# Second block's softmax on VectorE, low parts later, a fifth buffer for gated tiles: a fused attention and gating kernel

## The chip, the cores and the metric

The kernel runs on one core of a Trainium2 chip. Measured is the device time of one execution, in microseconds (us). A run gives one time; several runs of the same kernel are compared by their median. One further execution was profiled, and all rows below come from it.

## The reference

Attention inside chunks of 64 tokens, then two dense layers with a gate, then two more with a squared clip:

```python
scores = scale * np.matmul(q_c, k_c.transpose(0, 1, 2, 4, 3))   # chunks of 64, D = 64, 8 heads
scores = scores - np.max(scores, axis=-1, keepdims=True)
attn = np.exp(scores)
attn = attn / (np.sum(attn, axis=-1, keepdims=True) + 1e-09)
out = np.matmul(attn, v_c)
# x: 4608 tokens x 512 (heads side by side)
gate = 1.0 / (1.0 + np.exp(-(x @ w_gate)))                       # 512 -> 1536
val = x @ w_val
y = gate * val @ w_out                                           # 1536 -> 512
h = y @ w_in                                                     # 512 -> 2048
g = np.where(h >= 1, h, np.where(h <= -1, 0.0, (h + 1) ** 2 / 4))
return g @ w_out2                                                # 2048 -> 512
```

Inputs and output are float32.

## The kernel before

**Numbers.** Matrix products run on float32 operands that are split into a high and a low part. `three` issues three matmuls for one product (high by high, high by low, low by high; the lines L501, L502 and L503). `x` is the high part, a copy on ScalarE (L419), and `l` the low part, a subtraction on VectorE (L423).

**Blocks.** The 4608 tokens are nine blocks of 512. For every block the first stage computes the attention of its four pairs of heads, and then 12 pairs of products of 512 columns: gate, sigmoid on ScalarE (L905), value, and the product of both on VectorE (L908) into the tile `sg`, which SyncE (SP) stores to DRAM (`gT`, L791). One gate or value product is 12 matmuls of 128x512. Later stages read `gT` and compute the other three layers; they are not touched by the change and begin at about 745 us.

**Slots.** The first stage is written as a program by slots. A block has NS = 24 slots; each is one gate or value product on TensorE, gate in the even and value in the odd slots. `at(slot, prio, fn)` books a step, and `emit(slot)` writes all booked steps of that slot ahead of its product, by fraction of the slot, then by `prio`. What each engine runs, and in which order, follows from that alone: an engine takes its instructions in the written order, and waits for semaphores at each. All DMAs are issued by SP in the written order too.

**Attention beside the products.** `first_block` computes block 0's attention alone (0 to 36 us). For the others, `later_block(b, starts, when)` books the steps of pair p at slot `starts[p]` plus an offset for each of `tsmenwpcoxl`: transposes of q and k on VectorE (t, L306), scores on TensorE (s, L323), maximum (m), exponential on ScalarE (e), sums and reciprocal on VectorE (n), scaling of the weights on GpSimd (w, L383), transposes on TensorE (p, L389), their copy on ScalarE (c, L392), product with v on TensorE (o, L403), high parts (x), low parts (l). Loads of q and k are booked with `starts[p - 1]` (L281, 16 DMAs for a pair in blocks 1 to 7), those of v with `starts[p]` (L296). Block 1, the second, is computed beside block 0's products, in which VectorE, ScalarE and GpSimd also convert the weights (L111, L117, L124, L128, L137, L138).

**Softmax of block 1 before.** Only this block has a form of its own. `m_scaled` takes the maxima on VectorE (L347) and multiplies them by -scale (L348). `e_sums` runs eight exponentials of 128x64 on ScalarE straight from the scores, each with its maximum as the bias and each summing its row (L359). All other blocks subtract the maxima on VectorE (L339, four instructions), take one exponential of 128x512 (L367) and sum on VectorE (L375).

**Buffers.** The tile `sg` has four buffers, so the sigmoid of product pair f writes the buffer of pair f-4 and waits until that store has landed. The store of pair f, whose gate is in slot 2f, is booked in slot 2f + 4.

**Weights of later stages.** From slot 26 on, weights of the later layers are loaded (L102, L106), converted and written back to DRAM (L182), also by SP, beside the attention.

Of the kernel before, what the change touches and what calls it, by code (L numbers as in the profile page):

```python
# [8 lines left out]
F32 = mybir.dt.float32  # L9
F32R = mybir.dt.float32r  # L10
# [3 lines left out]
AF = mybir.ActivationFunctionType  # L14
ALU = mybir.AluOpType
AX = mybir.AxisListType
# [12 lines left out]
def kernel(  # L29
# [207 lines left out]
    class Whole:  # L237
# [88 lines left out]
            self.B["s", p] = banks  # L326

        def m(self, p):
            if self.b == 1:
                return self.m_scaled(p)  # L330
            s = self.SP[p][:, 0].rearrange("p (g h k) -> p g h k", h=2, k=CH)
            m = cp.tile([P, 2, NC], F32, tag="m0", name="m", bufs=2)
            banks = self.B.pop(("s", p))
            for h, b in enumerate(banks):
                nc.vector.tensor_reduce(out=m[:, h], in_=b, axis=AX.X, op=ALU.max)
            for h, b in enumerate(banks):
                for swap in range(2):
                    gs = slice(swap * NC // 2, (swap + 1) * NC // 2)
                    nc.vector.tensor_tensor(  # L339
                        out=s[:, gs, h ^ swap], in0=b[:, gs],  # L340
                        in1=m[:, h, gs].unsqueeze(2).to_broadcast([P, NC // 2, CH]), op=ALU.subtract,
                    )

        def m_scaled(self, p):
            m = cp.tile([P, 2, NC], F32, tag="m1", name="m", bufs=2)
            for h, b in enumerate(self.B["s", p]):
                nc.vector.tensor_reduce(out=m[:, h], in_=b, axis=AX.X, op=ALU.max)  # L347
            nc.vector.tensor_scalar_mul(m, m, -scale)  # L348
            self.B["m", p] = m

        def e_sums(self, p):

            s = self.SP[p][:, 0].rearrange("p (g h k) -> p g h k", h=2, k=CH)
            self.B["l", p] = l = cp.tile([P, NC, 2], F32, tag="l1", name="l", bufs=2)
            m = self.B.pop(("m", p))
            for h, b in enumerate(self.B.pop(("s", p))):
                for g in range(NC):
                    r = h ^ (g >= NC // 2)
                    nc.scalar.activation(  # L359
                        s[:, g, r], b[:, g], AF.Exp, bias=m[:, h, g:g + 1], scale=scale,  # L360
                        accum_out=l[:, g, r:r + 1],
                    )

        def e(self, p):
            if self.b == 1:
                return self.e_sums(p)
            nc.scalar.activation(self.SP[p][:, 0], self.SP[p][:, 0], AF.Exp, scale=scale)  # L367

        def n(self, p):
            if self.b == 1:  # L370
                l = self.B.pop(("l", p)).rearrange("p g h -> p (g h)")
            else:
                s = self.SP[p][:, 0].rearrange("p (g k) -> p g k", k=CH)
                l = cp.tile([P, 2 * NC], F32, tag="l0", name="l", bufs=2)
                nc.vector.tensor_reduce(out=l, in_=s, axis=AX.X, op=ALU.add)  # L375
            nc.vector.tensor_scalar_add(l, l, 1e-9)
            self.B["r", p] = r = cp.tile([P, 2 * NC], F32, tag="r0", name="r", bufs=2)
            nc.vector.reciprocal(out=r, in_=l)
# [46 lines left out]
    def first_block():  # L425
# [24 lines left out]
                    wl(1)  # L450
                n -= fn not in (w_low, w_bits)

        z = pool["sg"].tile([P, BS], F32R, tag="sg", name="z", bufs=4)
        nc.vector.memset(f32(z), 0.0)
        kv_["ident"] = cp.tile([P, P], F32, name="ident")
        make_identity(nc, kv_["ident"])
# [25 lines left out]
    def later_block(b, starts, when):  # L482

        bufs = {"qk": 2, "qkT": 1, "sp": 2, "vd": 2}

        def alloc(nm):
            cols = BS // 2 if nm == "vd" else BS
            return pool["u"].tile([P, 2, cols], F32, tag=nm, name=nm, bufs=bufs[nm])

        a = Whole(b, [None, "b4", "b5", "b6", "b6", "b7"], alloc, "V" * KT)  # L490
        for p, s0 in enumerate(starts):
            at(starts[p - 1] + 0.5 if p else s0 - 6, 5, a.load, p)
            at(s0 + 0.5, 5, a.v_load, p)
            for fn, dt in zip("tsmenwpcoxl", when):
                at(s0 + dt, {"s": 0, "p": 0, "o": 0, "m": 1, "e": 1, "c": 1, "x": 1}.get(fn, 3), getattr(a, fn), p)
# [294 lines left out]
    def g_store(b, f, sg):  # L790
        nc.sync.dma_start(out=gT[b][f * P:(f + 1) * P, :], in_=sg)  # L791

    later_block(1, [5 * p for p in range(KT)], (0, 1, 1.5, 2, 3, 3, 5, 5.5, 7, 7.5, 8))
    for b in range(2, NB):
        later_block(
            b, [NS * (b - 1) + 6 * p - 6 for p in range(KT)], (0, 2, 3, 3.5, 4, 4.5, 6, 7, 8, 9, 10)
# [83 lines left out]
    with tc.manual_schedule():  # L880
# [18 lines left out]
        for b in range(NB):  # L899
            for f in range(F1):  # L900
                slot = NS * b + 2 * f
                emit(slot)
                go = proj(("g", f), b, f"b{f % 2}")
                sg = pool["sg"].tile([P, BS], F32, tag="sg", name="sg", bufs=4)
                nc.scalar.activation(sg, go, AF.Sigmoid)  # L905
                emit(slot + 1)
                vo = proj(("v", f), b, f"b{2 + f % 2}")
                nc.vector.tensor_tensor(out=sg, in0=vo, in1=sg, op=ALU.mult)  # L908
                at(slot + 4, 7, g_store, b, f, sg)
        for t in range(3):  # L910
            emit(NS * NB + t)
        close_pool("sg")
        assert not ev, ev
# [38 lines left out]
```

## Time and profile before

| | us |
|---|---|
| median of 3 runs | 1727.68 |
| lowest, highest | 1726.67, 1732.06 |
| the profiled execution | 1730.08 |
| its span, from first to last instruction | 1728.3 |
| TensorE busy | 1658.0 |
| VectorE, ScalarE, GpSimd busy | 1188.6, 876.9, 834.6 |
| mean granted clock of TensorE | 0.988 |

Matmuls overlap in TensorE, so its busy time says when it is not idle, not that it runs at its peak. In the rows, PE is TensorE, PEld its weight loads, DVE VectorE, ACT ScalarE, POOL GpSimd and SPq the queue of SyncE. `L423` is line 423 of the kernel. "A <- B" in a wait is: A stood idle until B had ended.

### The profile page before, as it was taken

Reading aid. Unit: us, or ns where it says so; the run is one execution under the profiler, and the core shown is the slowest. Engines: PE = TensorE matmul, PEld = TensorE weight load, DVE = VectorE, ACT = ScalarE, POOL = GpSimd, SP = SyncE. Lnnn points to the kernel's source line nnn. Section 1 sums busy time; section 2 is a strip of 40 time slices with the busy share of each in tenths; the row PEclk is TensorE's granted clock in tenths of the full one; section 3 lists DMA queues with packets and bytes.
Section 4 is the critical chain, followed back from the end, with each engine's and each line's share of the span. In section 5 each row is a group of like instructions: output and inputs, shape, how many; then the busy total and the mean of one; then the engine's idle time right before and its main releaser. Section 6 shows DMA issues by size and latency. Waiting matters only on the chain.

```text
span 1728.3 us, 30194 instructions
## 1 busy us (share of the span) xinstructions
PE 1658.0 (96%) x10695; PEld 1525.4 (88%) x10695; DVE 1188.6 (69%) x1856; ACT 876.9 (51%) x1694; POOL 834.6 (48%) x755
## 2 busy tenths in 40 slices
PE   5889999998999899999999999999999999999998
PEld 4668887776877788899999999999999999999998
DVE  5875556555555562178777767888787879788876
ACT  5664455444454453145555555555554455545453
POOL 1431433433333241057777753533450476777675
PEclk8899999999999999999999999999999999999999
DMA  7655767777776875834654654333427954463452
GB/s 209 189 128 135 214 176 215 214 210 205 197 204 186 241 225 172 320 105 152 218 158 145 240 216 153 122 134 138 156 102 278 345 194 115 114 183 109 120 138 37
DMA packets 385991, 307.16 MB, mean 178 GB/s; under 512 B 267696, under 2 KB 298928, under 8 KB 385840
## 3 DMA queue, kind: packets, MB, share of 16 engines
q1 hardware_dynamic: 385840, 305.23, 57.6%
q8 instruction: 84, 1.38, 0.3%
q14 instruction: 67, 0.55, 0.1%
HBM read 179.83 MB, written 125.30 MB: 177 GB/s over the span
## 4 chain that ended last, share of the span: by engine, by line
PE 77%; DMA 8%; SPq 7%; DVE 4%; ACT 2%; issue 2%; POOL 1%; DVEq 0%; ACTq 0%; POOLq 0%
PE P L502 18%; PE P L503 18%; PE P L501 18%; PE pr L501 7%; PE pr L502 7%; PE pr L503 7%; SPq L281 4%; DMA gT<-sg 2%; SPq L296 2%; DMA raw<-in_moe_w_gate_dram 1%; PE O L403 1%; DMA raw<-in_moe_w_in_dram 1%; DMA vd<-in_v_dram 1%; DVE z L534 1%; PE S L323 1%
## 5 line engine op out<-in xcount | busy, mean ns | idle before, releaser
L545 POOL TENSOR_TENSOR z<-z 128x384 fp32r<-128x384 f32 x305 | 355.9, 1189 | 313.7 <-ACT z L538 306.6
L502 PE MATMUL P<-z,w 128*128 128x384 f32 x1344 | 454.6, 338 | 4.1 <-POOL z L545 2.2
L501 PE MATMUL P<-z,w 128*128 128x384 f32 x1344 | 453.7, 338 | 0.0
L503 PE MATMUL P<-z,w 128*128 128x384 f32 x1344 | 453.4, 337 | 0.0
L501 PE MATMUL pr<-x,w 128*128 128x512 f32 x864 | 347.9, 403 | 0.0
L502 PE MATMUL pr<-x,w 128*128 128x512 f32 x864 | 340.5, 394 | 0.9 <-DVE x L423 0.9
L503 PE MATMUL pr<-x,w 128*128 128x512 f32 x864 | 339.9, 393 | 0.0
L538 ACT ACTIVATE z<-z 128x384 fp32r<-128x384 f32 x420 | 206.0, 521 | 178.9 <-DVE z L534 108.6
L545 POOL TENSOR_TENSOR op<-in,op 128x384 fp32r<-128x384 f32 x168 | 191.0, 1155 | 147.6 <-ACT op L538 146.9
L502 PEld LDWEIGHTS P<-z,w 128*128 128x128 f32 x1344 | 252.5, 188 | 7.2 <-POOL z L545 5.0
L501 PEld LDWEIGHTS P<-z,w 128*128 128x128 f32 x1344 | 252.4, 188 | 0.6 <-ACT z L538 0.2
L503 PEld LDWEIGHTS P<-z,w 128*128 128x128 f32 x1344 | 252.4, 188 | 0.0
L908 DVE TENSOR_TENSOR sg<-pr,sg 128x512 f32<-128x512 f32 x108 | 74.5, 690 | 257.4 <-PE pr L503 108.6
L905 ACT ACTIVATE sg<-pr 128x512 f32<-128x512 f32 x108 | 64.6, 598 | 300.3 <-PE pr L503 215.9
L501 PEld LDWEIGHTS pr<-x,w 128*128 128x128 f32 x864 | 164.7, 191 | 35.3
L503 PEld LDWEIGHTS pr<-x,w 128*128 128x128 f32 x864 | 164.3, 190 | 35.4
L502 PEld LDWEIGHTS pr<-x,w 128*128 128x128 f32 x864 | 164.7, 191 | 33.6 <-DVE x L423 1.4
L538 ACT ACTIVATE op<-in 128x384 fp32r<-128x384 f32 x252 | 128.5, 523 | 112.3 <-PE P L503 57.7
L534 DVE TENSOR_TENSOR z<-z 128x384 f32<-128x384 f32 x200 | 168.5, 892 | 1.0 <-POOL z L545 0.9
L502 PE MATMUL P<-op,w 128*128 128x384 f32 x504 | 168.5, 334 | 0.1
L501 PE MATMUL P<-op,w 128*128 128x384 f32 x504 | 168.5, 334 | 0.0
L503 PE MATMUL P<-op,w 128*128 128x384 f32 x504 | 168.4, 334 | 0.0
(68 smaller groups left out, 2257.4 us busy)
## 6 DMA issues: line engine op xcount, KB each, us to landing
uT<-ua SPq DMA_DIRECT2D x96, 384.0 KB, 2.3
z<-uT SPq DMA_DIRECT2D x96, 384.0 KB, 4.3
gT<-sg SPq DMA_DIRECT2D x108, 256.0 KB, 5.1
in<-gT SPq DMA_DIRECT2D x72, 256.0 KB, 3.9
raw<-in_moe_w_out_dram SPq DMA_DIRECT2D x28, 512.0 KB, 6.4
w<-swi SPq DMA_DIRECT2D x28, 512.0 KB, 5.7
w<-swp SPq DMA_DIRECT2D x28, 512.0 KB, 6.9
swi<-st SPq DMA_DIRECT2D x24, 512.0 KB, 4.1
```

Of the source, the lines that this page charges most:

```text
L281: nc.sync.dma_start(out=t[32 * g:32 * g + 32, i, off // 32:(off + m) // 32], in_=rows[h, :, 32 * j:32 * j + 32].rearrange("(t i) r -> i t ...
L296: nc.sync.dma_start(out=t[heads[h ^ swap], lo // CH:hi // CH], in_=v[bb, 2 * p + h, s0 + lo - off:s0 + hi - off].rearrange("(c k) d -> k c ...
L323: nc.tensor.matmul(banks[h][heads[c % 2], c // 2], lhsT=t[hs, 0, ts], rhs=t[hs, 1, ts], start=True, stop=True)
L403: nc.tensor.matmul(banks[r][heads[r ^ swap], g_, i], lhsT=self.V[p][rows, c], rhs=self.SP[p][rows, 1, chunks[c]], start=True, stop=True,)
L501: nc.tensor.matmul(o, lhsT=ah, rhs=bh, start=first, stop=False, skip_group_check=open_)
L502: nc.tensor.matmul(o, lhsT=ah, rhs=bl, start=False, stop=False, skip_group_check=open_)
L503: nc.tensor.matmul(o, lhsT=al, rhs=bh, start=False, stop=last, skip_group_check=open_)
L534: (eng or nc.vector).tensor_tensor(out=op_src(p, key), in0=x, in1=y, op=ALU.subtract)
L538: nc.scalar.activation(o[:, 0], op_src(p, key), AF.Copy)
L545: eng.tensor_tensor(out=o[:, 1], in0=op_src(p, key), in1=f32(o[:, 0]), op=ALU.subtract)
L905: nc.scalar.activation(sg, go, AF.Sigmoid)
L908: nc.vector.tensor_tensor(out=sg, in0=vo, in1=sg, op=ALU.mult)
```

## The change

Three things. Block 1's softmax takes the form of the other blocks: `m_scaled` and `e_sums` go. The tile `sg` (and `z`, which shares its buffers) has five buffers instead of four, and its store is booked in slot 2f + 3 instead of 2f + 4. In block 1 the last pair starts at slot 14 instead of 15, and the low parts of each pair come at offset 9 instead of 8.

```diff
         def m(self, p):
-            if self.b == 1:
-                return self.m_scaled(p)
...
-        def m_scaled(self, p):
-            m = cp.tile([P, 2, NC], F32, tag="m1", name="m", bufs=2)
-            for h, b in enumerate(self.B["s", p]):
-                nc.vector.tensor_reduce(out=m[:, h], in_=b, axis=AX.X, op=ALU.max)
-            nc.vector.tensor_scalar_mul(m, m, -scale)
-            self.B["m", p] = m
-
-        def e_sums(self, p):
...
-                    nc.scalar.activation(
-                        s[:, g, r], b[:, g], AF.Exp, bias=m[:, h, g:g + 1], scale=scale,
-                        accum_out=l[:, g, r:r + 1],
-                    )
...
-        z = pool["sg"].tile([P, BS], F32R, tag="sg", name="z", bufs=4)
+        z = pool["sg"].tile([P, BS], F32R, tag="sg", name="z", bufs=5)
...
-    later_block(1, [5 * p for p in range(KT)], (0, 1, 1.5, 2, 3, 3, 5, 5.5, 7, 7.5, 8))
+    later_block(1, [0, 5, 10, 14], (0, 1, 1.5, 2, 3, 3, 5, 5.5, 7, 7.5, 9))
...
-                sg = pool["sg"].tile([P, BS], F32, tag="sg", name="sg", bufs=4)
+                sg = pool["sg"].tile([P, BS], F32, tag="sg", name="sg", bufs=5)
...
-                at(slot + 4, 7, g_store, b, f, sg)
-        for t in range(3):
+                at(slot + 3, 7, g_store, b, f, sg)
+        for t in range(2):
```

VectorE, block 0, the second pair of block 1 and the low parts of the first, before:

```order
L347 TENSOR_REDUCE m<-S 128x4 x2
L348 TENSOR_SCALAR m<-m 128x8
L128 SCALAR_TENSOR_TENSOR raw<-raw 128x512
L111 TENSOR_SCALAR raw<-raw 128x512
L117 SCALAR_TENSOR_TENSOR raw<-raw 128x512
L908 TENSOR_TENSOR sg<-pr,sg 128x512
L423 TENSOR_TENSOR x<-O,x 64x256 x4
L376 TENSOR_SCALAR l<-l 128x8
L378 RECIPROCAL r<-l 128x8
L128 SCALAR_TENSOR_TENSOR raw<-raw 128x512
```

and after, where the lines are numbered lower (L333 and L337 are the maxima and the subtraction, L348 to L351 sum and reciprocal, L396 the low parts, L881 the gated product):

```order
L333 TENSOR_REDUCE m<-S 128x4 x2
L337 TENSOR_TENSOR sp<-S,m 128x2x64 x4
L128 SCALAR_TENSOR_TENSOR raw<-raw 128x512
L111 TENSOR_SCALAR raw<-raw 128x512
L117 SCALAR_TENSOR_TENSOR raw<-raw 128x512
L881 TENSOR_TENSOR sg<-pr,sg 128x512
L348 TENSOR_REDUCE l<-sp 128x8
L349 TENSOR_SCALAR l<-l 128x8
L351 RECIPROCAL r<-l 128x8
L128 SCALAR_TENSOR_TENSOR raw<-raw 128x512
L111 TENSOR_SCALAR raw<-raw 128x512
L117 SCALAR_TENSOR_TENSOR raw<-raw 128x512
```

The low parts have moved behind the sum, the reciprocal and one more weight (the next row after these is L396).

SP's queue, block 0, around the loads for the second and third pair of block 1 (gT_66 is block 0's), before:

```order
L102 DMA raw<-in_moe_w_val_dram 128x4x128
L791 DMA gT_66<-sg 128x512
L102 DMA raw<-in_moe_w_gate_dram 128x4x128
L296 DMA vd<-in_v_dram 64x64 x2
L296 DMA vd<-in_v_dram 64x3x64 x2
L296 DMA vd<-in_v_dram 64x4x64 x2
L281 DMA qk<-in_q_dram 32x2x32 x4
```

and after:

```order
L764 DMA gT_66<-sg 128x512
L102 DMA raw<-in_moe_w_val_dram 128x4x128
L102 DMA raw<-in_moe_w_gate_dram 128x4x128
L764 DMA gT_66<-sg 128x512
L296 DMA vd<-in_v_dram 64x64 x2
L296 DMA vd<-in_v_dram 64x3x64 x2
L296 DMA vd<-in_v_dram 64x4x64 x2
L281 DMA qk<-in_q_dram 32x2x32 x4
```

The store of product pair 1, which stood behind six loads of v, 16 of q and k and a weight, now stands ahead of them.

## Rows read from the trace of the kernel before

**Rows 1.** Busy time by engine, behind the first stretches: stretch, length, engine busy.

```profile
582.00:750.00 168.00, 168.00 (x1019) 139.02 (x1019) 61.56 (x124) 59.20 (x104) 39.83 (x40) 1.00 0.70 230
```

**Rows 2.** Waits of TensorE, 36 to 130 us: total, times, longest.

```profile
PE S L323 <- DVE qkT L306: 9.9, 4, 5.0
PE PT L389 <- POOL sp L383: 7.4, 3, 2.6
```

**Rows 3.** VectorE's waits, 36 to 130 us; timeline rows of one period: start, duration.

```profile
DVE x L423 <- ACT x L419: 13.2, 4, 3.9
...
71.37 0.51 DVE L348 TENSOR_SCALAR m<-m 128x8 f32<-128x8 f32 x1
...
77.95 1.53 DVE L423 TENSOR_TENSOR x<-O,x 64x256 fp32r<-64x256 f32 x4 [3.56 <-ACT x L419]
...
80.05 1.38 POOL L383 TENSOR_TENSOR sp<-sp,r 128x512 f32<-128x512 f32 x1 [2.47 <-DVE r L378]
```

**Rows 4.** Waits of TensorE and of ScalarE, 250 to 582 us.

```profile
PE O L403 <- ACT sp L392: 23.4, 10, 4.8
...
ACT sg L905 <- DMA gT<-sg: 84.0, 14, 10.4
```

**Rows 5.** Waits of SP, 36 to 152 us; the last row 152 to 600 us.

```profile
SPq L791 <- DVE sg L908: 5.3, 2, 3.4
...
SPq L791 <- DVE m L335: 2.8, 1, 2.8
...
SPq L296 <- PE O L403: 1.0, 1, 1.0
...
SPq L791 <- DVE sg L908: 1.5, 3, 0.7
```

**Rows 6.** Timeline of SP, block 6: start, duration, issues.

```profile
552.49 5.65 SPq L296 DMA_DIRECT2D vd<-in_v_dram  x6
558.18 4.08 SPq L281 DMA_DIRECT2D qk<-in_q_dram  x8
...
567.74 1.20 SPq L791 DMA_DIRECT2D gT<-sg  x2
```

**Rows 7.** Groups by line (busy us, mean ns): ScalarE and VectorE, 36 to 582 us.

```profile
L359 ACT ACTIVATE sp<-S,m 128x64 f32<-128x64 f32 x32 | 9.6, 324 | 0.0
...
L367 ACT ACTIVATE sp<-sp 128x512 f32<-128x512 f32 x23 | 14.6, 633 | 0.3
...
L339 DVE TENSOR_TENSOR sp<-S,m 128x128 f32<-128x128 f32 x96 | 20.9, 278 | 0.0
...
L375 DVE TENSOR_REDUCE l<-sp 128x8 f32<-128x512 f32 x23 | 15.8, 686 | 2.7 <-ACT sp L367 1.8
```

**Rows 8.** Busy time in two stretches; third last number: TensorE's granted clock.

```profile
103.20:106.60 3.40, 3.28 (x10) 2.80 (x11) 3.24 (x4) 0.70 (x1) 1.50 (x2) 0.50 0.81 183
574.30:581.10 6.80, 6.29 (x74) 5.27 (x75) 3.53 (x9) 1.59 (x3) 1.95 (x3) 0.50 0.91 257
```

**Rows 9.** Timeline of SP, six v pieces at two places; the product of pair 1.

```profile
55.56 6.76 SPq L296 DMA_DIRECT2D vd<-in_v_dram  x6
...
62.45 0.68 DVE L908 TENSOR_TENSOR sg<-pr,sg 128x512 f32<-128x512 f32 x1
...
132.28 3.88 SPq L296 DMA_DIRECT2D vd<-in_v_dram  x6
```

**Rows 10.** Timeline of VectorE, TensorE and ScalarE around the last long wait.

```profile
549.21 0.71 DVE L306 STREAM_TRANSPOSE qkT<-qk 128x512 f32<-128x512 f32 x1 [2.35 <-DMA qk<-in_k_dram]
...
552.05 0.65 PE L323 MATMUL S<-qkT 64*64 64x64 f32 x32
...
573.67 0.60 ACT L905 ACTIVATE sg<-pr 128x512 f32<-128x512 f32 x1 [10.36 <-DMA gT<-sg]
...
574.81 1.14 PE L403 MATMUL O<-sp,vd 64*64 64x64 f32 x32 [4.54 <-ACT sp L392]
...
581.80 0.60 ACT L905 ACTIVATE sg<-pr 128x512 f32<-128x512 f32 x1 [5.91 <-PE pr L503]
```

More of the change, by code (lines that the diff above doesn't have):

```diff
@@ L342, in m @@
                     )
-        def m_scaled(self, p):
-            m = cp.tile([P, 2, NC], F32, tag="m1", name="m", bufs=2)
-            for h, b in enumerate(self.B["s", p]):
-                nc.vector.tensor_reduce(out=m[:, h], in_=b, axis=AX.X, op=ALU.max)
-            nc.vector.tensor_scalar_mul(m, m, -scale)
-            self.B["m", p] = m
-        def e_sums(self, p):
[L353 to L358, printed above, removed]
-                    nc.scalar.activation(
-                        s[:, g, r], b[:, g], AF.Exp, bias=m[:, h, g:g + 1], scale=scale,
-                        accum_out=l[:, g, r:r + 1],
-                    )
         def e(self, p):
-            if self.b == 1:
-                return self.e_sums(p)
             nc.scalar.activation(self.SP[p][:, 0], self.SP[p][:, 0], AF.Exp, scale=scale)
         def n(self, p):
[L370 to L375, printed above, removed]
+            s = self.SP[p][:, 0].rearrange("p (g k) -> p g k", k=CH)
+            l = cp.tile([P, 2 * NC], F32, tag="l0", name="l", bufs=2)
+            nc.vector.tensor_reduce(out=l, in_=s, axis=AX.X, op=ALU.add)
             nc.vector.tensor_scalar_add(l, l, 1e-9)
```

## The prediction

> **What bounds the kernel now.** I read the waits of TensorE by stretch first, then asked for each waiting engine what it waits for, and ended at the queue of SP, which issues every DMA. TensorE stands idle in two stretches of the attention-and-gating stage only; behind 582 us it is busy in all of 168 us [rows 1], so work before that point shifts the end one for one if it shifts TensorE at all.
>
> First stretch, 36 to 130 us (block 0, with the attention of the second block beside it): TensorE waits 9.9 us for the transposed q and k and 7.4 us for the weights that GpSimd has scaled [rows 2]. What ends these waits is VectorE's order. In one period it stands 3.56 us before the low parts (L423), because the copies of the high parts (L419) stand behind the exponentials on ScalarE; four such waits make 13.2 us; only then come the sums' small operations and the scaling on GpSimd at 80.05 [rows 3], on which TensorE waits three times, 7.4 / 3 = 2.5 us each [rows 2].
>
> Second stretch, 250 to 582 us: TensorE waits 23.4 us for the copy L392, ten times, and that copy stands behind sigmoids that wait 84.0 us for stores of earlier gated tiles to land [rows 4], since the tile of product f (the f-th pair of gate and value products, 0 to 107) takes the buffer of f-4. So far this says: too few buffers. But why do the stores land late? SP waits in 36 to 152 us for gated products, maxima and TensorE (5.3, 2.8 and 1.0 us); in 152 to 600 us it waits 1.5 us for gated products [rows 5]. In that second time its rows stand end to end: 552.49 + 5.65 = 558.14, and the next begins at 558.18; the two stores at 567.74 come behind these six pieces of v and the loads of q and k [rows 6].  The store is late because SP has not come to it, not because the product isn't there. **SP's issue is the wall from 152 to about 580 us**: what it does there starts when the previous issue ends, whatever TensorE does.
>
> **Part 1, maxima and sums.** Per pair of heads, ScalarE loses the eight exponentials with their sums and gains one exponential of 633 ns; 32 of the small ones kept it busy for 9.6 us, so eight for 2.4 us, and 1.8 us go [rows 7]. VectorE loses the scaling of the maxima (0.51 us [rows 3]) and gains four subtractions (4 x 278 ns, 0.87 us as they overlap) and a sum of 686 ns [rows 7]: 0.87 + 0.69 - 0.51 = 1.05 us more, 4.2 us for four pairs. VectorE has room for it in the 13.2 us of waits for the copies [rows 3].
>
> **Part 2, low parts at +9, last pair at slot 14.** The sum and reciprocal (at +3) of the next pair now stand ahead of the low parts, not behind them. The scaling on GpSimd needs maximum, subtraction, exponential, sum; with the durations above it is ready some 2 to 4 us before TensorE asks for it, where it came 2.5 us too late. So the three waits for GpSimd go, 7.4 us, and with them two half-speed stretches that follow two of them (3.4 us at a granted clock of 0.50, the lower level of 1.2 GHz; one of the two in [rows 8]), worth 1.7 us each: 10.8 us. Of the 9.9 us before the scores, 5.0 us is the first pair's, whose loads and work are not changed; the other 4.9 us may shrink or grow, because those transposes stand in VectorE's order behind the 1.05 us per pair. I take 10 us, between 5 (VectorE eats half) and 15 (all 4.9 us go too).
>
> **Part 3, stores one slot earlier on SP.** A store holds everything behind it until its product is made. One place costs: the store of product 1 now stands ahead of six v pieces and 16 loads of q and k that were issued from 55.56 us, while its product ended at 62.45 + 0.68 = 63.1 us and should now end about 61: some 5.5 us of waiting. But those six v pieces took 6.76 us behind weight loads still in flight, where six take 3.88 us at 132.28 [rows 9], and the q loads behind them were slow too: some 4 us come back, 1.5 us are lost. Later stores in block 0 find their product done.
>
> **What SP gains.** The waits for computation up to 152 us are 5.3 + 2.8 + 1.0 = 9.1 us [rows 5]. TensorE being 10 us earlier, they go; less the 1.5 us, SP enters the long stretch 7.5 us earlier. More it cannot gain there: its work is the same. Bounds 3 us (VectorE late, so that part of the waits stays) and 9.
>
> **Part 4, the fifth buffer.** A sigmoid now waits for the store of f-5. The one at 573.67, the last long wait, is followed on TensorE by 4.54 us of idle and a half-speed stretch of 6.8 us (3.4 us lost) [rows 8, 10]. With the older store it is free. What is late next are the loads of q and k, which come from the same queue: the second transpose at 549.21 waited for its load, ended at 549.92, and the scores ran at 552.05, so this pair can come 2.1 us earlier against SP and no more [rows 10]. On the way from there to 574.81 TensorE loses 4.54 us that go: 6.6 us; with the clock 10.0 us; and the next sigmoid, at 581.80, needs the stores issued at 567.74, which had landed at 573.6, so 8.2 us is the cap. I take 8.0 us, between 2 (other loads, of v or of weights, bind at once) and 10. The earlier waits of the stretch count for nothing of their own: TensorE catches up with SP after each.
>
> **Rule against row.** The rows show both a gap that comes back on TensorE [rows 4] and an issue queue without gaps [rows 6]. The Trainium skill, page "Perfetto Trace Analysis", section "Optimization Strategy", says that a gap repeating on the engine that should be saturated can mean too little room for the next tile, buffer count among it; by that rule alone the fifth buffer takes all these gaps, and the time is that of the second rival. The same page, section "What 'DMA-bound' means", counts an issuing sequencer that is solid with DMA slices as a bound of its own, which more buffers do not lift; by that the sum above stands. Rows 5 and 6 are nearer to the second.
>
> **Sum.** 7.5 + 8.0 = 15.5 us off a span of 1728.3 us; the profiled execution took 1730.08 us in all and the median of the runs is 1727.68. 1727.68 - 15.5 = 1712.2 us.
>
> **Rivals.**
> 1. The first stretch gives nothing: VectorE's added 4.2 us and its place ahead of the transposes eat what the sums gain. SP starts the long stretch as before and only the buffer counts, 8 us: 1719.7. For it: VectorE is the busiest helper in block 0. Against it: those 13.2 us of idle.
> 2. SP is no wall, only a symptom: the stalls go with the buffer. 23.4 us [rows 4], the 3.4 us of the last half-speed stretch [rows 8] and 10 us of block 0: 1727.7 - 36.8 = 1690.9 (shorter half-speed stretches behind earlier stalls would add to it). Against it: 1.5 us of waits in 448 us [rows 5].
> 3. Nothing to measure: the loads behind the stores bind at once and block 0 gives about as much as the stores' waits cost SP: 1727.7, within 5 us of it.
> 4. Slower: VectorE is the bound of block 0. Each pair's 1.05 us delays the next transposes, 4.2 us in all, SP waits the longer for its products, and with stores ahead of loads it also loses what it had issued ahead, up to 8 us at one place (16 loads at the half microsecond of [rows 6], an estimate; I take half of it), less the 2 us of the buffer's lower bound: 4.2 + 4 - 2 = 6 us, 1734. It decides if the transposes of the third and fourth pair (before the waits for VectorE in [rows 2]) come later than before.
>
> **How the numbers follow.** Chances: forecast 0.57, rival 1 0.18, rival 2 0.07, rival 3 0.11, rival 4 0.07. The forecast's own bounds are 3 + 2 = 5 and 9 + 10 = 19 us; with rival 1 inside and the others left out at the ends, 1705 to 1722 holds 8 in 10. About 0.3% (5.2 us) is what a measurement of this kernel can tell from no change. Faster: 0.57 x 0.97 + 0.18 x 0.85 + 0.07 = 0.78; slower 0.07; the rest, 0.15, within.
>
> **What would show it.** Right: no wait of TensorE for GpSimd in block 0; SP's waits for products gone after some 65 us; sigmoids waiting for stores far less than 84 us between 250 and 580 us, but TensorE waiting instead for VectorE's transposes, and those for the loads of q and k, with 10 to 25 us of TensorE idle left there; SP still end to end. Wrong: TensorE without idle in 250 to 580 us (rival 2), the transposes of block 0 no earlier (rivals 1 and 4), or SP waiting for products in 150 to 250 us as before.

## The result, and the profile after

The changed kernel takes 1713.9 us (median of 4, 1709.95 to 1717.25) where the kernel before took 1729.8 beside it: a ratio of 0.9911, 95% interval 0.9894 to 0.9928, some 15.4 us off. The forecast was 1712.2 us, with 1705 to 1722 as the range. The time agrees; the sum behind it does not quite, and most of what follows is about that.

Line numbers after are 27 lower from the copies on: L396 are the low parts (L423 before), L392 the copies of the high parts (before, L392 is the copy of PT, which is now L365), L881 the gated product, L764 the store, L362 PT, L376 the product with v, L474 to L476 the three matmuls.

Busy time by stretch (length, then TensorE, its weight loads, VectorE, ScalarE, GpSimd; the third last number is the granted clock), first before, then after:

```profile
36.00:130.00 94.00, 75.57 (x565) 59.06 (x566) 72.05 (x125) 62.02 (x148) 36.38 (x27) 0.93 0.60 155
250.00:582.00 332.00, 305.61 (x2328) 248.22 (x2327) 180.52 (x379) 154.07 (x262) 126.91 (x132) 0.97 0.72 202
```

```profile
36.00:130.00 94.00, 77.99 (x606) 61.23 (x607) 78.00 (x146) 58.92 (x95) 37.14 (x27) 0.91 0.62 158
250.00:582.00 332.00, 315.86 (x2337) 254.92 (x2330) 183.10 (x389) 163.26 (x275) 129.96 (x134) 0.98 0.71 202
```

TensorE's idle between 250 and 582 us has gone from 26.4 to 16.1 us, but in 36 to 130 us it is 16.0 us where it was 18.4. What TensorE waits for after, first from 36 to 130 us, then from 250 to 582 us (waiting instruction, what ended the wait, us, times, longest):

```profile
PE PT L362 <- DVE x L396: 8.9, 3, 6.1
PE S L323 <- DVE qkT L306: 6.0, 3, 5.0
```

```profile
PE PT L362 <- POOL sp L356: 7.9, 11, 3.0
PE S L323 <- DVE qkT L306: 6.3, 4, 3.0
PE O L376 <- DMA vd<-in_v_dram: 2.0, 2, 1.0
```

In block 0 the waits for GpSimd of [rows 2] are gone; in their place stand 8.9 us for the low parts, one of them 6.1 us. In the long stretch the waits for the copy of PT (23.4 us in [rows 4], ten of them) are gone, and TensorE waits for GpSimd's scaling and the transposes of q and k instead. The sigmoids, which waited 84.0 us for stores to land [rows 4], wait for no store of theirs any more; what they wait for is TensorE, here in the first row. The second is VectorE's at one of the waits for q and k (2.2 us before the scores at 382.43) and names what it waits for, the load:

```profile
ACT sg L878 <- PE pr L476: 97.3, 28, 10.4
...
381.66 0.71 DVE L306 STREAM_TRANSPOSE qkT<-qk 128x512 f32<-128x512 f32 x1 [3.31 <-DMA qk<-in_k_dram]
```

Three places make a ledger of where time goes: the end of the product of VectorE that closes block 0 (product 11), of the one that closes the stage (product 107), and the end of the program. All are from the VectorE rows of the gated product in each profile; "rest" is from product 107 to the end. The runs below are in it too.

| kernel | product 11 | product 107 | 11 to 107 | rest | ratio to before (95%) |
|---|---|---|---|---|---|
| before | 138.1 | 746.2 | 608.1 | 982.1 | 1 |
| changed | 135.3 | 732.8 | 597.5 | 975.4 | 0.9911 (0.9894 to 0.9928) |
| buf_only | 139.6 | 738.2 | 598.6 | 983.8 | 0.9957 (0.9941 to 0.9974) |
| soft_only | 135.4 | 743.5 | 608.1 | 975.4 | 0.9953 (0.9939 to 0.9968) |
| buf6 | 137.9 | 737.4 | 599.5 | 977.5 | 0.9911 (0.9885 to 0.9937) |
| gap128 | 136.6 | 735.3 | 598.7 | 981.9 | 0.9948 (0.9931 to 0.9964) |
| low8 | 140.4 | 743.4 | 603.0 | 976.9 | 0.9927 (0.9909 to 0.9944) |
| last15 | 134.7 | 742.3 | 607.6 | 978.2 | 0.9944 (0.9927 to 0.9960) |
| pt_b4 | 141.6 | 742.0 | 600.4 | 977.1 | 0.9941 (0.9927 to 0.9956) |
| copy7 | 138.6 | 741.8 | 603.2 | 975.4 | 0.9930 (0.9906 to 0.9955) |
| store2 | 136.2 | 732.9 | 596.7 | 975.1 | 0.9882 (0.9861 to 0.9902) |
| store_act | 144.4 | 742.8 | 598.4 | 976.6 | 0.9948 (0.9929 to 0.9967) |
| qk_fat | 136.3 | 712.0 | 575.7 | 976.8 | 0.9776 (0.9761 to 0.9790) |
| fat_all | 136.4 | 712.1 | 575.7 | 975.4 | 0.9771 (0.9751 to 0.9792) |

Of the 20.1 us between the two profiles' spans, 2.8 us are block 0, 10.6 us the stretch up to product 107, and 6.7 us lie in later stages that the change does not touch. The changed kernel's profile is its fastest run; three kernels of its order (changed, buf6, gap128) close the stage at 732.8, 737.4 and 735.3 us, so one profile is good to some 4 us there.

Product 11 is TensorE's place, not SP's. Where SP stands is told by transfers that all these kernels share: the loads of v for the third pair of block 2 (before, then after) and for the third pair of block 7 (after; before it is the 552.49 of [rows 6]):

```profile
151.25 4.11 SPq L296 DMA_DIRECT2D vd<-in_v_dram  x6
...
148.38 4.20 SPq L296 DMA_DIRECT2D vd<-in_v_dram  x6
...
546.98 5.65 SPq L296 DMA_DIRECT2D vd<-in_v_dram  x6
```

SP's way from the first place to the second takes 401.2 us before, 398.6 in the changed kernel, 400.2 in buf_only, 402.4 in soft_only, 400.9 in buf6 and 400.3 in gap128. From the second place to product 107 it is 193.7 and 192.6 us with four buffers (before, soft_only) and 185.3 to 185.8 in the four kernels with more. So the fifth buffer leaves SP's way as it is and takes some 8 us off behind it.

### The profile page after: what moved, and what is told of

Read it like the earlier page. It is cut to its first block, busy times and chain, and to the rows that moved or that the text cites. A ratio compares the mean times of both kernels' runs of the same rounds, so it can differ in the third digit from the quotient of the medians.

```text
span 1708.2 us, 30165 instructions
## 1 busy us (share of the span) xinstructions
PE 1649.3 (97%) x10695; PEld 1514.1 (89%) x10695; DVE 1195.8 (70%) x1872; ACT 870.2 (51%) x1634; POOL 835.2 (49%) x755
## 4 chain that ended last, share of the span: by engine, by line
PE 73%; DVE 9%; SPq 7%; DMA 5%; issue 2%; POOL 2%; ACT 1%; DVEq 0%; POOLq 0%; ACTq 0%
PE P L475 17%; PE P L474 17%; PE P L476 17%; PE pr L474 7%; PE pr L475 7%; PE pr L476 7%; SPq L281 4%; DVE z L507 2%; SPq L296 1%; DVE raw L128 1%; DMA raw<-in_moe_w_val_dram 1%; DMA swp<-st 1%; DVE z L518 1%; PE O L376 1%; DVE x L396 1%
## 5 line engine op out<-in xcount | busy, mean ns | idle before, releaser
L474 PE MATMUL P<-z,w 128*128 128x384 f32 x1344 | 449.4, 334 | 0.0
L476 PE MATMUL P<-z,w 128*128 128x384 f32 x1344 | 449.1, 334 | 0.0
L474 PE MATMUL pr<-x,w 128*128 128x512 f32 x864 | 347.8, 403 | 0.0
L476 PE MATMUL pr<-x,w 128*128 128x512 f32 x864 | 339.9, 393 | 0.0
L474 PEld LDWEIGHTS P<-z,w 128*128 128x128 f32 x1344 | 252.3, 188 | 0.8 <-ACT R L533 0.3
L476 PEld LDWEIGHTS P<-z,w 128*128 128x128 f32 x1344 | 252.3, 188 | 0.0
L881 DVE TENSOR_TENSOR sg<-pr,sg 128x512 f32<-128x512 f32 x108 | 74.5, 690 | 209.7 <-PE pr L476 126.7
L476 PEld LDWEIGHTS pr<-x,w 128*128 128x128 f32 x864 | 164.3, 190 | 35.7
L474 PEld LDWEIGHTS pr<-x,w 128*128 128x128 f32 x864 | 164.5, 190 | 35.0
L507 DVE TENSOR_TENSOR z<-z 128x384 f32<-128x384 f32 x200 | 172.5, 912 | 1.0 <-POOL z L518 0.9
L476 PE MATMUL P<-op,w 128*128 128x384 f32 x504 | 168.4, 334 | 0.0
L474 PE MATMUL P<-op,w 128*128 128x384 f32 x504 | 168.4, 334 | 0.0
```

The lines of the kernel that those rows point to most:

```text
L474: nc.tensor.matmul(o, lhsT=ah, rhs=bh, start=first, stop=False, skip_group_check=open_)
L476: nc.tensor.matmul(o, lhsT=al, rhs=bh, start=False, stop=last, skip_group_check=open_)
L507: (eng or nc.vector).tensor_tensor(out=op_src(p, key), in0=x, in1=y, op=ALU.subtract)
```

## The two parts alone

buf_only adds to the kernel before only the fifth buffer and the earlier store:

```diff
-                sg = pool["sg"].tile([P, BS], F32, tag="sg", name="sg", bufs=4)
+                sg = pool["sg"].tile([P, BS], F32, tag="sg", name="sg", bufs=5)
...
-                at(slot + 4, 7, g_store, b, f, sg)
+                at(slot + 3, 7, g_store, b, f, sg)
...
```

> Fifth buffer and the store one slot earlier, the second block's softmax as before. Theory (SP's issue is the wall, the fifth buffer frees TensorE up to it): block 0 as before, SP enters the long stretch at the same time as in the kernel before (within 2 us), and the sigmoids' waits for stores go between 250 and 582 us; TensorE then waits for loads of q and k instead, and the time is 8 to 11 us shorter than before, ratio 0.9936 to 0.9954. Rival (the buffer alone makes the whole gain, the softmax none): 13 to 16 us shorter, ratio 0.9907 to 0.9925. Rival (the buffer helps only together with the earlier block 0): 0 to 3 us, ratio above 0.998.

Measured: 0.9957, 7.4 us, just under the theory's range. The stage ends 8.0 us earlier: block 0 is 1.5 us later and the stretch from product 11 on 9.5 us shorter. The waits in 250 to 582 us are for the same things as in the changed kernel, none of them for the copy:

```profile
PE PT L389 <- POOL sp L383: 9.1, 12, 2.9
PE S L323 <- DVE qkT L306: 9.0, 5, 3.4
PE O L403 <- DMA vd<-in_v_dram: 1.6, 2, 0.9
```

soft_only is the changed kernel with those lines as before (the softmax, offset 9 and slot 14 remain).

> The second block's softmax on VectorE, low parts at offset 9 and the last pair at slot 14, but four buffers and the store in slot 2f + 4. Theory: the end of block 0 is some 3 us earlier as in the changed kernel, SP is 3 us earlier through the long stretch, the sigmoids still wait for stores that SP issues late, and TensorE's waits for the copy L365 stay; the time is 2 to 4 us shorter, ratio 0.9977 to 0.9988. Rival (the stalls of the long stretch take up what block 0 gives): 0 to 1 us. Rival (without the earlier store SP waits less in block 0, so that the lead is larger): 5 to 8 us, ratio 0.9954 to 0.9971.

Measured: 0.9953, 8.1 us, at the upper end of the last rival's range, yet not for its reason: the stage ends only 2.7 us earlier, all of it in block 0, and the stretch behind takes 608.1 us as before. Its waits in 250 to 582 us are still those for the copy:

```profile
PE O L376 <- ACT sp L365: 22.1, 10, 4.3
PE PT L362 <- POOL sp L356: 2.7, 7, 0.8
```

The other 6.7 us are in the rest, 975.4 us against 982.1. So the parts add up (0.9957 x 0.9953 = 0.9910), but the softmax brings most of its share where it does nothing. That is taken up in "The rest of the program".

## Is SP's queue the wall?

Four runs ask this. buf6 has six buffers (a filler tile is 768 bytes smaller to make room):

```diff
...
-                sg = pool["sg"].tile([P, BS], F32, tag="sg", name="sg", bufs=5)
+                sg = pool["sg"].tile([P, BS], F32, tag="sg", name="sg", bufs=6)
```

> The changed kernel with six buffers for the gated tiles (and a filler tile 768 bytes smaller to make room). Theory (with five buffers the sigmoids no longer wait for stores; what is late are the loads of q and k): the first stage ends within 1.5 us of the changed kernel's 732.8 us, TensorE's idle in 250 to 582 us stays at 14 to 18 us, ratio to before 0.990 to 0.993. Rival (too few buffers is what leaves the 16.1 us of idle): idle falls below 8 us, the stage ends 6 to 12 us earlier, ratio 0.984 to 0.988.

Measured: the same ratio, 0.9911, and 17.6 us of idle in 250 to 582 us. The stage ends at 737.4, not within 1.5 us of 732.8, but 2.6 of these 4.6 us are there at product 11. A sixth buffer brings nothing.

qk_fat loads q and k of blocks 2 to 8 in rows of 256 elements, all in few transfers:

```diff
+                    elif self.b > 1:
+                        nc.sync.dma_start(
+                            out=t.rearrange("p i t r -> p i (t r)")[part, i].rearrange("i (h e) -> i h e", h=2),
+                            in_=rows.rearrange("h (i j) d -> i h (j d)", j=NC),
+                        )
```

> The changed kernel, in which blocks 2 to 8 load q and k of a pair in 4 transfers (2 where a block lies in one sequence... 4 where it crosses into the next) instead of 16: the same bytes, laid out so that the transposes put them in the wrong places, so the attention of these blocks is not the reference's; all else is kept. Theory (the order of SP's transfers is the wall from 152 to 580 us, each taking some 0.45 to 0.5 us there however small it is): some 12 fewer per pair give SP 5 us of every 18, it waits for computation everywhere behind block 1, TensorE's waits for q and k (6.3 us) and with them those for GpSimd's scaling and v go, its idle in 250 to 582 us falls below 5 us, the first stage ends 12 to 20 us earlier than 732.8 us and the ratio to before is 0.979 to 0.985. Rival (the bytes bind, not the number of transfers): the loads land as late as before, within 3 us of the changed kernel, ratio 0.990 to 0.993. Rival (behind SP stands GpSimd or VectorE): the waits for loads go, those of TensorE for GpSimd's scaling stay at 7 us or more, 5 to 9 us earlier.

Measured: 1690.6 us, 0.9776, 23 us less than the changed kernel and a little beyond the theory's range; the stage ends at 712.0. TensorE's waits in 250 to 582 us, all there are, and then SP's longest in 152 to 580 us:

```profile
PE PT L367 <- POOL sp L361: 2.0, 6, 0.3
```

```profile
SPq L769 <- DVE sg L886: 135.1, 38, 6.4
```

Idle fell from 16.1 to 2.0 us, and SP, which waited 1.5 us for gated products before (152 to 600 us, [rows 5]), waits 135.1 us for them. The rival by which GpSimd's scaling would stay late falls: its 7.9 us went with the loads. The same bytes move, so bytes are not it. But the transfers are not only fewer, their contiguous pieces are longer as well (256 elements in place of 32), and this run can't part the two.

store_act takes the stores off SP and keeps them in the same places of the written order:

```diff
-        nc.sync.dma_start(out=gT[b][f * P:(f + 1) * P, :], in_=sg)
+        nc.scalar.dma_start(out=gT[b][f * P:(f + 1) * P, :], in_=sg)
```

> The changed kernel with the 108 stores of gated tiles issued by ScalarE, not by SP. Theory (SP's issue is the wall from 152 to 580 us): each store takes SP 0.45 to 0.9 us, so a block's twelve give it back 5 to 10 us, it runs ahead of TensorE within two blocks and waits for computation; the transposes no longer wait for loads of q and k, TensorE's 16.1 us of idle between 250 and 582 us fall below 6 us, and the time is 8 to 16 us shorter than the changed kernel's, ratio to before 0.982 to 0.987. Rival (the DMA engines' transfers bind, not the issue): TensorE waits for the same loads, time within 3 us of the changed kernel's, ratio 0.990 to 0.993. Rival (ScalarE, held by stores that wait for VectorE's product, becomes late for sigmoids and copies): slower than the changed kernel, TensorE waiting for ScalarE, ratio above 0.995.

Measured: 0.9948, slower than the changed kernel and in none of the three ranges. In block 0 TensorE loses 9.1 us (product 11 at 144.4), which speaks for the last rival. But in the long stretch its idle is 17.4 us and the loads are as late as ever, though SP's issues from 152 to 580 us took 326.7 us where they took 375.9. What SP got back it waits away:

```profile
SPq L281 <- DMA gT<-sg: 23.6, 12, 3.9
SPq L296 <- DMA raw<-in_moe_w_out_dram: 11.7, 11, 1.9
SPq L296 <- DMA gT<-sg: 10.6, 3, 5.2
```

A load of q that waits for a store of gated tiles to land has no data to get from it. The records show what it is: the transfers signal eight semaphores in turn, and each but the first eight waits for the one that it will signal itself, so for the eighth transfer before it, in written order and across both engines. Among the landings that the records hold, no issue between 152 and 580 us ended less than 0.33 us after the eighth transfer before it had landed, in any of these kernels, while the seventh before was still under way in 2 to 11 of 100. This lies in the program's semaphores.

In the changed kernel it binds little: from 152 to 580 us SP waits 11.3 us for transfers to land; in store_act it is 70.5. So SP's issue time is the wall, as I had put it, but the ordered row stands close behind: a store issued elsewhere stays a place in that row, and what SP no longer issued it waited away. Its way between the two loads of v is 403.2 us. The Trainium skill, page "Perfetto Trace Analysis", section "DMA Optimizations", says that spreading transfers over several issuing engines may help where issuing is the limit; in this kernel that brought nothing in the stretch, 17.4 us of idle against 16.1. The same page of the Trainium skill, section "What 'DMA-bound' means", counts a solid issuing sequencer as a bound of its own, for which large descriptors are what matters; qk_fat, with longer pieces, agrees by its 23 us. That more buffers do not lift such a bound is not on the page; buf6 shows it for this kernel.

store2 takes half of the stores out of the row, with two gated tiles in one (three buffers of two, so room for six tiles, which by itself brought nothing in buf6):

```diff
...
-                sg = pool["sg"].tile([P, BS], F32, tag="sg", name="sg", bufs=5)
+                if f % 2 == 0:
+                    sg2 = pool["sg"].tile([P, 2, BS], F32, tag="sg", name="sg", bufs=3)
+                sg = sg2[:, f % 2]
...
-                at(slot + 3, 7, g_store, b, f, sg)
+                if f % 2:
+                    at(slot + 3, 7, g_store, b, f - 1, sg2)
```

> The changed kernel with one store for two gated tiles (three buffers of two tiles in place of five of one; the store stands where the second tile's stood). Theory (the number of SP's transfers is the wall): between 152 and 580 us 32 transfers fewer, at 0.53 us each some 17 us of SP's 428; TensorE's waits for loads of q and k shrink, and the first stage ends 6 to 14 us earlier than the changed kernel's (732.8 and 737.4 us in two profiles of its order), ratio to before 0.982 to 0.988. Rival (a store of twice the size holds the queue as long as two, because the eighth transfer before must have landed): within 3 us, ratio 0.989 to 0.993. Rival (the store of two tiles waits longer for its product and holds up the loads behind it in block 0): slower than the changed kernel by 2 to 6 us.

Measured: 1710.4 us, 0.9882, the fastest here that computes the reference, 5 us below the changed kernel by the ratios, though the intervals overlap a little. From product 11 to 107 it takes 596.7 us against 597.5 to 599.5 in the three of the changed order. That is 1 to 3 us, not the 17 us that SP's time would make. Between the two loads of v there are 30 stores fewer, and SP issues stores for 15.2 us there in place of 31.7 to 34.1. But the other transfers take longer to issue, so that all of them take 343.6 us in place of 348.7 to 352.0, and the waits for landings in 152 to 580 us grow from 11.3 to 21.7 us. Why the others take longer is open: a store of two tiles is not slower to land in the median (4.3 us against 3.3 to 4.3 in the three of the changed order).

## What holds block 0

TensorE was 10 us ahead at product 6 (95.6 us against 106.0), and 2.8 us at product 11. It lost most of the lead in one wait and the half-speed stretch around it, here in the rows of TensorE, VectorE and ScalarE:

```profile
104.72 0.69 PE L376 MATMUL O<-sp,vd 64*64 64x64 f32 x32
117.14 1.09 PE L362 MATMUL PT<-ident,sp 128*128 128x128 f32 x4 [6.05 <-DVE x L396]
```

```profile
109.96 0.43 DVE L111 TENSOR_SCALAR raw<-raw 128x512 int32<-128x512 uint32 x1 [0.78 <-DMA raw<-in_moe_w_gate_dram]
110.43 1.67 DVE L117 SCALAR_TENSOR_TENSOR raw<-raw 128x512 int32<-128x512 int32 x1
...
115.47 1.52 DVE L396 TENSOR_TENSOR x<-O,x 64x256 fp32r<-64x256 f32 x4
```

```profile
112.18 0.67 ACT L124 ACTIVATE raw<-raw 128x512 f32<-128x512 f32 x1 [2.19 <-DVE raw L117]
112.75 1.29 ACT L392 ACTIVATE x<-O 64x256 fp32r<-64x256 f32 x4
```

PT of the last pair writes the PSUM bank b6, which the third pair's low parts still read (the bank list of `later_block` has b6 for PT and for half of O). The low parts wait for the copies, the copies for a weight's scaling, that for VectorE, and VectorE for a weight that SP loaded late. I tried each link.

low8 puts the low parts back to offset 8, last15 the last pair to slot 15:

```diff
-    later_block(1, [0, 5, 10, 14], (0, 1, 1.5, 2, 3, 3, 5, 5.5, 7, 7.5, 9))
+    later_block(1, [0, 5, 10, 14], (0, 1, 1.5, 2, 3, 3, 5, 5.5, 7, 7.5, 8))
```

> The changed kernel with the low parts at offset 8 again. In the changed kernel TensorE was 10 us ahead of before at the third pair and lost 6.05 us at 117.14 us, where the transposes of the last pair's weights waited for the low parts of the third pair (both use the PSUM bank b6), and a half-speed stretch behind it. Theory (the low parts at offset 9 stand too late on VectorE for the bank): the wait of 6.05 us shrinks to under 2.5 us, SP enters the long stretch 4 to 6 us earlier than in the changed kernel and the time is 4 to 7 us shorter than the changed kernel's, ratio to before 0.987 to 0.989. Rival (the sums, again behind the low parts, bring back the waits for GpSimd): TensorE waits 2 to 2.5 us three times for the scaled weights, the time within 2 us of the changed kernel's, ratio 0.990 to 0.992.

```diff
-    later_block(1, [0, 5, 10, 14], (0, 1, 1.5, 2, 3, 3, 5, 5.5, 7, 7.5, 9))
+    later_block(1, [0, 5, 10, 15], (0, 1, 1.5, 2, 3, 3, 5, 5.5, 7, 7.5, 9))
```

> The changed kernel with the second block's last pair at slot 15 again, low parts at offset 9. Theory (the wait of 6.05 us at 117.14 comes from the last pair's transposes, in slot 19, standing ahead of the third pair's low parts, in the same slot, for the PSUM bank b6): at slot 20 the transposes find the bank free or nearly, the wait falls below 2.5 us and no half-speed stretch follows it; the first stage ends 4 to 7 us earlier than in the changed kernel (732.8 us), at 726 to 729, ratio to before 0.986 to 0.989. Rival (the wait moves to the pair's later steps, or to the scores of the next block, because everything of the pair is a slot later): within 2 us of the changed kernel's, the stage ends at 731 to 735. Rival (SP, not TensorE, sets what block 0 hands on): block 0 is 4 us earlier for TensorE, the stage's end within 2 us.

Both came out slower, 0.9927 (its interval overlaps the changed kernel's) and 0.9944, and close the stage at 743.4 and 742.3. In low8 the longest wait for low parts shrank to 3.2 us, but TensorE's waits for the transposes of q and k rose from 6.0 to 12.0 us, where VectorE stood waiting for copies ahead of them (9.2 us in 36 to 130 us, where it was 1.9). In last15 the wait stayed, 5.23 us at 118.43, and the pair's low parts, now in the next block, held PT there for another 2.37 at 136.25: product 11 was the earliest of all (134.7), and the stretch behind it 10 us longer than in the changed kernel. SP had gained nothing by the early product: it is at the loads of v of block 2 at 151.9 us, 3.6 us later than in the changed kernel, and its way takes 404.6 us, 6.0 us more. Why the way is longer was not tried.

pt_b4 gives PT another bank, copy7 puts the copies ahead of the weights on ScalarE:

```diff
-        a = Whole(b, [None, "b4", "b5", "b6", "b6", "b7"], alloc, "V" * KT)
+        a = Whole(b, [None, "b4", "b5", "b4", "b6", "b7"], alloc, "V" * KT)
```

> The changed kernel with the transposed weights (PT) of blocks 1 to 8 in the PSUM bank b4, which the scores have left by then, not in b6, which the low parts still read. Theory (the bank is what the 8.9 us of three waits in block 0 come from): TensorE waits for no low parts, TensorE is 6 to 10 us earlier at 140 us than in the changed kernel, SP's waits for gated products in block 0 shrink, and the first stage ends 5 to 9 us earlier than 732.8 us, at 724 to 728, ratio to before 0.985 to 0.988. Rival (the next waits stand right behind: the scaling on GpSimd and the loads of q and k): 2 to 4 us, ratio 0.988 to 0.991. Rival (the scores of the next pair now wait for ScalarE's copy out of b4): TensorE waits for the copy L365 in each pair, slower than the changed kernel.

```diff
-    later_block(1, [0, 5, 10, 14], (0, 1, 1.5, 2, 3, 3, 5, 5.5, 7, 7.5, 9))
+    later_block(1, [0, 5, 10, 14], (0, 1, 1.5, 2, 3, 3, 5, 5.5, 7, 7, 9))
```

> The changed kernel with the copies of the second block's high parts (L392) at offset 7 in place of 7.5. On ScalarE they then stand ahead of that slot's weight scaling and split, right behind the sigmoid of the slot before; in the changed kernel the third pair's copies began at 112.75 us, though its product with v had ended at 105.4. Theory (TensorE's 8.9 us of waits for low parts in block 0 come from these late copies): the copies of the third pair start some 5 us earlier against the product with v, the waits for low parts shrink to under 3 us, TensorE is 5 to 8 us earlier at the end of block 0 and the first stage ends 5 to 9 us earlier than in the changed kernel (732.8 and, with six buffers and the same order, 737.4 us), ratio to before 0.985 to 0.988. Rival (ScalarE now waits for the product with v, and the exponentials behind it are late): the waits move to GpSimd's scaled weights, 0 to 5 us slower, ratio 0.991 to 0.994. Rival (SP's order sets what block 0 hands on, through the weights it loads late): within 2 us, ratio 0.990 to 0.992.

0.9941 and 0.9930. What TensorE waits for in 36 to 140 us, first in pt_b4, then in copy7:

```profile
PE S L323 <- ACT sp L365: 15.0, 4, 6.1
PE S L323 <- DVE qkT L306: 5.0, 1, 5.0
```

```profile
PE PT L362 <- DVE x L396: 9.6, 3, 3.5
PE S L323 <- DVE qkT L306: 6.1, 3, 5.0
```

With the bank free the wait changes its name and grows: the last rival of pt_b4, scores waiting for ScalarE's copy out of b4. In copy7 the third pair's copies stand 3.1 us behind the start of their product with v instead of 8.0, as meant, and that product itself comes 5.9 us later (110.63 against 104.72); the waits for low parts are 9.6 us, evenly spread.

fat_all takes the last link away, SP's late weights (qk_fat with `self.b > 0`).

> As the kernel with q and k of blocks 2 to 8 in 4 transfers per pair, but block 1 too (so the attention of blocks 1 to 8 is not the reference's; all else is kept). It takes 48 transfers, some 25 us, out of SP's queue in block 0. Theory (SP's queue is the wall in block 0 as well: the weights' transfers at 105.28 us stood behind 16 loads, landed late at 109.9, and VectorE, ScalarE, the low parts and TensorE's wait of 6.05 us hang on them): that wait falls below 3 us, TensorE is 4 us or more earlier at 140 us, and the stage ends 4 to 8 us earlier than the 712.0 us of the kernel with blocks 2 to 8 alone, ratio to before 0.973 to 0.976. Rival (the order on VectorE and ScalarE makes the wait, whatever SP does): within 2 us of that kernel, ratio 0.9765 to 0.979, the waits for low parts stay at 7 to 10 us.

The stage ends at 712.1, qk_fat's at 712.0; the waits for low parts are 8.6 us. So the rival holds: SP does not make these waits. The four moves of steps and bank cost 3 to 6 us by the ratios (the intervals of low8 and copy7 overlap the changed kernel's; the stage ends at 741.8 to 743.4 in all four, after the 732.8 to 737.4 of its order), none came out as its theory had it, and relief on SP brought nothing. The suspect that is left is how full VectorE is. The stretch 60 to 110 us, before and after (the third busy time is VectorE's):

```profile
60.00:110.00 50.00, 40.07 (x308) 31.06 (x307) 39.53 (x68) 32.32 (x78) 19.75 (x15) 0.93 0.68 179
```

```profile
60.00:110.00 50.00, 46.15 (x371) 36.25 (x370) 46.51 (x90) 35.11 (x55) 21.98 (x16) 0.97 0.68 180
```

Its idle went from 10.5 to 3.5 us in 50, in part because TensorE was ahead and more of the work fell into the stretch (371 matmuls in place of 308). In low8 the moved step stands in front of something else that TensorE needs. But VectorE as the bound of block 0 is argued, not shown, and it does not fit pt_b4, where VectorE is busy for 39.4 of these 50 us and TensorE waits for ScalarE. A block 0 with less work for VectorE was not tried; what holds it stays open.

## The rest of the program

Behind product 107 the instructions are the same, TensorE is idle for 4 to 6 us, the granted clock is 0.995 to 1.00, and yet the kernels with the old softmax take 982.1 to 983.8 us and those with the new one, but for the run below, 975.1 to 978.2. The change removes two small tiles (`m` and `l` of the old form, 128 bytes per partition), and the pools behind theirs in SBUF begin 128 bytes lower. gap128 is the changed kernel with that place filled again:

```diff
-        half = cp.tile([P, 1], F32, name="half")
+        gap, half = cp.tile([P, 32], F32, name="gap"), cp.tile([P, 1], F32, name="half")
```

> The changed kernel with one unused tile of 128 bytes per partition in the pool that held the two small tiles of the old softmax (their place, 128 bytes, has gone with the change), so that the pools behind it in SBUF, among them the one of the last stages' operands, begin where they began before. The instructions are the changed kernel's. Behind 950 us the profiles of the kernel before and of the one with the fifth buffer alone show TensorE solidly busy at 337 to 341 ns a matmul of 384 columns, those of all kernels with the new softmax 334 to 335 ns. Theory (the placement of these tiles makes the difference): TensorE's matmuls behind 950 us take 337 to 341 ns again, the time from the end of the first stage to the end of the program is 981 to 984 us where the changed kernel has 975.4, and the kernel is 5 to 8 us slower than the changed kernel, ratio to before 0.994 to 0.997. Rival (the instructions that ScalarE no longer has make it): 975 to 978 us and ratio 0.990 to 0.993.

Measured: 0.9948, and 981.9 us for the rest. TensorE in 300 us of that stage, the kernel before, gap128 and the changed kernel in turn (its count of matmuls is in the first brackets):

```profile
1060.00:1360.00 300.00, 300.00 (x1716) 300.00 (x1715) 237.42 (x328) 163.73 (x306) 110.83 (x97) 1.00 0.45 172
```

```profile
1048.80:1348.80 300.00, 300.00 (x1716) 300.00 (x1715) 237.50 (x327) 163.68 (x307) 111.22 (x97) 1.00 0.45 171
```

```profile
1040.00:1340.00 300.00, 300.00 (x1733) 300.00 (x1732) 241.48 (x331) 166.64 (x314) 112.35 (x98) 1.00 0.45 171
```

Always busy at a granted clock of 1.00, and 1716 or 1733 matmuls. The placement makes it, not ScalarE's instructions. By the ratios it is 0.9948 - 0.9911 = 0.0037, 6.4 us of the 15.4; by the profiles 981.9 - 975.4 = 6.5. The groups of matmuls (busy us, mean ns) tell which products it touches, those of `z`: before, gap128, changed; those of `op`, in the last row before, take 334 ns in all three.

```profile
L502 PE MATMUL P<-z,w 128*128 128x384 f32 x1344 | 454.6, 338 | 4.1 <-POOL z L545 2.2 <-DVE z L545 1.7
...
L475 PE MATMUL P<-z,w 128*128 128x384 f32 x1344 | 455.8, 339 | 4.1 <-POOL z L518 2.2 <-DVE z L518 1.7
...
L475 PE MATMUL P<-z,w 128*128 128x384 f32 x1344 | 450.5, 335 | 5.1 <-POOL z L518 3.1 <-DVE z L518 1.7
...
L502 PE MATMUL P<-op,w 128*128 128x384 f32 x504 | 168.5, 334 | 0.1
```

## Where the prediction was right and where not

**SP as the wall, and the fifth buffer: right.** Forecast were 8.0 us from the buffer, all of them at the end of SP's long stretch. Behind SP's loads of v of block 7 the stage takes 193.7 us before and 185.3 to 185.8 in changed, buf_only, buf6 and gap128, 7.9 to 8.4 us less; the way up to there is the same within some 3 us. What was to be late next, the loads of q and k, is what TensorE now waits for, with 16.1 us of idle where 10 to 25 were said. Rival 2, by which SP is a symptom, is out: a sixth buffer brings nothing. One reading was too good: the 1.5 us of [rows 5] are one row of many. All of SP's waits from 152 to 580 us add up to 37 us before and 34 after, 14 and 11 of them for transfers to land; SP issues for 375 and 376 of the 428 us.

**Part 3: right.** In the changed kernel SP issues the six pieces of v at 61.19 us, 5.6 later than the 55.56 of [rows 9], and is back by the next six, at 78.39 where it was 78.94.

**Block 0: wrong, and the step that failed is in part 2.** The waits for GpSimd went as worked out (7.4 us to none), and TensorE was 10 us ahead at product 6. But "I take 10 us, between 5 and 15" is 2.8 us in the profile of the changed kernel and 0.2 and 1.5 in the two others of its order. The two half-speed stretches, 3.4 us of the 10.8, did not go: one is at 79.1 us now, and one twice as long stands in and behind the 6.05 us of wait:

```profile
113.20:120.00 6.80, 2.86 (x9) 2.50 (x10) 4.43 (x10) 3.93 (x8) 2.72 (x2) 0.50 0.33 83
```

Two things were missed. The low parts free the bank that PT needs, so moving them later had a taker on TensorE whom the text didn't name. And "VectorE has room for it in the 13.2 us of waits": in 60 to 110 us it had 10.5 us of idle, and 3.5 were left. Whether VectorE was the bound, as rival 4 had it, stays open; what is shown is that a gain of 10 us became one of 0 to 3.

**SP's entry: wrong by the same.** 7.5 us were forecast (9.1 - 1.5 is 7.6). At the loads of v of block 2 SP is 2.9 us earlier in the changed kernel, 0.2 in buf6 and 1.6 in gap128, all under the lower bound of 3. SP's waits for gated products between 36 and 152 us did not go:

```profile
SPq L764 <- DVE sg L881: 8.5, 3, 3.1
```

They are 8.5 us where 5.3 were, 5.5 of them behind 65 us, from where on they were to be gone. With the earlier store alone it is 10.6 us (buf_only), with the softmax alone still 6.2 (soft_only). Nothing was gained by that slot in block 0: in buf_only product 11 is 1.5 us late.

**The sum: right for part of the reason, the rest is luck.** 15.5 us were to come out of the first stage. There came 13.4, 8.8 and 10.9 us in the profiles of the three kernels of this order, about 11, and 6.5 us from a placement that no step looked at and that happened to fill the gap. Without it the kernel takes 1720.5 us (gap128), which is rival 1's case: the first stretch gives next to nothing, the buffer 8 us, 1719.7.

## What to carry to other kernels

A part that was forecast right should be looked for in its own stretch: a total that agrees can hold a missing 4.5 us and a found 6.5. Where one engine's queue is the wall, measure from a place in that queue, not from the engine that waits for it. When a step is moved on a busy engine, list who waits for the buffers that it frees, and count the idle time of that engine in the stretch, not over the kernel. Where the issuing of one row of transfers is the wall, 240 fewer ones between the two loads of v, with longer pieces, brought 23 us; stores in pairs brought 1 to 3, a sixth buffer and another issuing engine nothing.

## What was not expected of the hardware

128 bytes of SBUF placement changed the pace of a TensorE that was hardly ever idle: the 4032 matmuls of 128x384 with `z` take 334 to 335 ns on average with the pools lower, 337 to 339 with them as before, which is the 6.5 us in 980. In the stretches shown, all matmuls of the changed kernel start 173 or 174 ns after the one before; in gap128 and before, 13 of 100 start more than 178 ns after it. Which tile it is and why was not tried.

Of the program and not of the chip, but as little expected: a wait on TensorE for data can hang on transfers that have nothing to do with it, because each transfer waits for the eighth before it, whichever engine issues it.
